# Sorted attention and a gated FFN on one core: gate weights issued one copy earlier, a narrower spreading matrix, and a new order of the last key, value and score steps of the first batch

## The chip, the core and the metric

The kernel runs on one NeuronCore of a Trainium2 chip. The core has TensorE for matmuls (weight loads are listed apart as PEld), VectorE (DVE), ScalarE (ACT), GpSimd (POOL) and SyncE (SP), and 16 DMA engines. The metric is device time in microseconds (us) of one execution. Before the change it is 244.59 us, the median of three runs (244.46 to 245.49). All times inside the text that have no other unit are us from the start of the profiled span.

## The reference

Four batches of eight heads hold 768 rows of 64 in eight blocks of 96 rows. A small 8x8 matrix per head is made doubly stochastic by five rounds of exponential, row normalisation and column normalisation. It mixes whole blocks of keys and of values, then each block of queries attends to its mixed block, and the result goes through a gated feed-forward layer of width 1536.

```
P = sort_net                                  # [4, 8, 8, 8]
for _ in range(5):
    P = exp(P - max(P)); P /= sum(P, rows); P /= sum(P, columns)
k_sorted = einsum('bhij,bhjcd->bhicd', P, k)  # the same for v
attn = softmax(q @ k_sorted.T / 8) per block of 96
x = (attn @ v_sorted) as [3072, 512]
out = (silu(x @ w_gate) * (x @ w_val)) @ w_out
```

## The kernel before, in words

All matmul operands are bf16; loads from float32 cast on their way through GpSimd's DMA queue. The work has a short opening stage and a long feed-forward stage. The feed-forward (`ffn`, with `gate`, `value` and `outp`) goes in eight steps of 384 tokens, each 12 chunks of 128 gate and value columns. While one step runs, `merge` slips the attention of a later half batch between its matmuls, at due times written into the lists. TensorE's, GpSimd's, ScalarE's and SyncE's order is the order of the program text; VectorE's is too in the opening stage, up to the first exit from the manual schedule (L583), and is chosen by the planner afterwards.

The opening stage handles the first half of batch 0. GpSimd's queue holds, in this order: the loads of batch 0's values (L131, two halves), an identity matrix, the first load of queries (L168), the two halves of the keys (L175), three copies (`copy_v`, L150) that turn values from row order into column order in `vch`, and then the weights' loads: gate and value columns 0 to 256, the second load of queries, columns 256 to 512, 512 to 1024, 1024 to 1536, and then more inputs. ScalarE copies the rest of the values between the rounds of the 8x8 normalisation (L218 to L235), whose other steps are VectorE's. The memset that puts ones into the value tile of batch pair 1 (`vt_tile(1)`) lies in the third round.

The last product of the rounds (L236) writes the matrix eight times side by side into `p_bf`. For each of eight rows two matmuls with 64 columns (L494) then spread it over 128 partitions of `w_ps`, and VectorE makes block mixing matrices `rmix` of it. Value chunks (`v_chunk`, matmuls at L300, eight or sixteen of the 64 value columns each) and key chunks (`k0_chunk`, matmuls at L284, eight or sixteen rows each) multiply by `rmix`, and a cast on VectorE ("v", L242) or ScalarE ("s", L244) moves each out of PSUM. The last two key chunks cast their first 16 blocks at once and the rest later. Then come the scores (`qk`, L332, with the exponentials at L343 or L345), the value products (`av`, L359, with a reciprocal L363 and a product L365 on VectorE), the transposes (`x_first`, L376) and the first gate and value matmuls (`early`, L559). `fill` and `wide_fill` (L477, L481) are matmuls on zeros whose results nobody reads.

PSUM has eight banks, given out under tags: "gen" is three banks in rotation, "x" one, "a" and "b" a pair of banks each. A tile under a tag waits until the last reader of the tile that held the bank is done. `k0_chunk` with 16 rows takes a pair, with eight rows one bank. `qk` under "gen" takes two single banks and makes two exponentials of 384 elements; under "a" or "b" it takes the pair and makes one of 768.

## Time and profile before

| | |
|---|---|
| median of three runs | 244.59 us (244.46, 244.59, 245.49) |
| the profiled execution | 243.93 us, span 242.2 |
| TensorE busy | 232.7 us, 96% of the span |
| VectorE busy | 155.6 us, 64% |
| ScalarE busy | 112.0 us, 46% |
| GpSimd busy | 54.9 us, 23% |
| granted TensorE clock | 1.000 |
| DMA | 24.76 MB, 102 GB/s in the mean |

The page of the profile cuts the span into 40 slices of 6.05 us and gives each engine's busy share in tenths. Its chain is the work that ended last, followed back from the end. A timeline line gives the start, the length, the engine, the line of the kernel, the operation, the output and inputs, their shape, a count where several are merged, and in brackets the idle time before it with what ended that. The list of waits gives the total, the count and the longest.

### The profile page before, as it was taken

To read this page: it belongs to the slowest core of one execution; us is meant where nothing else is said; L and a number is where in the kernel's file an instruction comes from. 1 tells how busy PE (TensorE), PEld (TensorE's weight loads), DVE (VectorE), ACT (ScalarE), POOL (GpSimd) and SP (SyncE) were. 2 spreads that over 40 slices of the span, in tenths; PEclk is the share of its full clock that TensorE was granted. 3 is DMA by queue.
4 is the path that set the end of the run, shared out by engine and by line. 5 is a ranking of instruction groups with operands and counts; after the bars stand their busy time and mean duration, and the time that the engine had idled before them with its cause. 6 is when DMAs were issued, how large, how long until landed. Compare 5 with 4: busy or idle time off the path is not lost.

```text
span 242.2 us, 5881 instructions
## 1 busy us (share of the span) xinstructions
PE 232.7 (96%) x2453; PEld 136.8 (56%) x2476; DVE 155.6 (64%) x327; ACT 112.0 (46%) x190; POOL 54.9 (23%) x66
## 2 busy tenths in 40 slices
PE   7789999999999999999999999999999999999994
PEld 3376665775556556555555565565556555555543
DVE  6796889874666585776855765484566477445700
ACT  3977652577526434455454253345325433332212
POOL 5997228970006089000000000000000000000000
PEclk9999999999999999999999999999999999999999
DMA  5989999999936999462122112012111211110122
GB/s 96 214 120 181 206 213 211 206 211 202 174 92 132 186 164 152 90 129 71 37 72 63 35 43 77 3 60 64 35 41 55 67 37 43 43 43 3 43 87 87
DMA packets 40698, 24.76 MB, mean 102 GB/s; under 512 B 29408, under 2 KB 35424, under 8 KB 40672
## 3 DMA queue, kind: packets, MB, share of 16 engines
q0 software_dynamic: 20688, 14.16, 41.2%
q1 hardware_dynamic: 19840, 10.17, 16.7%
q8 instruction: 19, 0.31, 0.5%
q10 hardware_dynamic: 144, 0.07, 0.1%
q14 instruction: 7, 0.06, 0.1%
HBM read 28.32 MB, written 7.86 MB: 149 GB/s over the span
## 4 chain that ended last, share of the span: by engine, by line
PE 85%; DMA 7%; POOL 5%; issue 1%; DVE 1%; ACT 0%; POOLq 0%
PE v_ps L428 25%; PE g_ps L410 25%; PE o_ps L445 24%; DMA wv_sb<-in_moe_w_val_dram 5%; POOL vch L150 3%; PE tkq L264 3%; PE av_ps L359 3%; PE qk L332 2%; DMA v<-in_v_dram 2%; PE tv L310 1%; PE o_ps L461 1%; POOL wg_sb L136 1%; PE tv L300 1%; POOL wv_sb L136 1%; PE x_ps L376 0%
## 5 line engine op out<-in xcount | busy, mean ns | idle before, releaser
L420 DVE SCALAR_TENSOR_TENSOR gs_sb<-th_sb,g_ps 128x384 bf16<-128x384 bf16 x96 | 52.9, 551 | 50.1 <-ACT th_sb L418 47.1
L410 PE MATMUL g_ps<-xt,wg_sb 128*128 128x384 bf16 x376 | 76.6, 325 | 0.1
L428 PE MATMUL v_ps<-xt,wv_sb 128*128 128x384 bf16 x376 | 76.5, 326 | 0.1
L418 ACT ACTIVATE th_sb<-g_ps 128x384 bf16<-128x384 f32 x96 | 47.1, 491 | 57.0 <-PE g_ps L410 54.3
L445 PE MATMUL o_ps<-wo,h 128*128 128x512 bf16 x254 | 61.4, 379 | 1.5 <-issue 0.5
L433 DVE SCALAR_TENSOR_TENSOR h<-v_ps,gs_sb 128x384 bf16<-128x384 f32 x96 | 53.4, 556 | 7.7 <-DVE gs_sb L420 0.5
L428 PEld LDWEIGHTS <-wv_sb 128*128 128x128 bf16 x376 | 35.0, 97 | 23.3 <-issue 0.2
L410 PEld LDWEIGHTS <-wg_sb 128*128 128x128 bf16 x376 | 34.9, 97 | 23.4
L445 PEld LDWEIGHTS <-h 128*128 128x128 bf16 x276 | 26.0, 98 | 28.5
L450 ACT COPY o_sb<-o_ps 128x512 f32<-128x512 f32 x23 | 13.5, 586 | 49.3 <-PE o_ps L445 49.3
L150 POOL COPY vch<-v 64x1536 bf16<-64x1536 bf16 (+2 forms) x11 | 29.4, 2712 | 9.8 <-PE g_ps L410 8.1
L345 ACT ACTIVATE e_all<-qk 96x768 bf16<-96x768 f32 x30 | 23.2, 801 | 3.8 <-PE qk L332 3.7
L365 DVE TENSOR_TENSOR st<-av_ps,r_sb 96x512 bf16<-96x512 f32 x32 | 21.8, 680 | 0.3
L359 PEld LDWEIGHTS <-e_all 96*128 96x128 bf16 x256 | 11.9, 97 | 4.6 <-ACT e_all L345 0.3
L359 PE MATMUL av_ps<-vt,e_all 96*128 96x65 bf16 x256 | 13.0, 193 | 0.2 <-ACT e_all L345 0.2
L244 ACT CAST vt<-tv 96x1024 bf16<-96x1024 f32 (+1 forms) x10 | 9.7, 965 | 4.9 <-PE tv L310 3.5
L363 DVE RECIPROCAL r_sb<-av_ps 96x8 f32<-96x8 f32 x32 | 6.4, 199 | 7.8 <-PE av_ps L359 7.8
L242 DVE CAST vt<-tv 96x1024 bf16<-96x1024 f32 (+1 forms) x8 | 8.0, 1016 | 2.1 <-PE tv L310 1.8
L481 PE MATMUL idle_ps<-wide_sb 128*128 128x512 f32 x8 | 6.4, 954 | 1.5 <-DVE wide_sb L70 1.5
L242 DVE COPY oq_v<-o_ps 128x128 f32<-128x128 f32 x1 | 0.3, 293 | 9.3 <-PE o_ps L461 9.3
L395 POOL DMA_DIRECT2D q_scr<-in_q_dram x2 | 5.6, 2813 | 0.3 <-issue 0.3
L332 PE MATMUL qk<-kqt 64*128 64x96 bf16 x128 | 4.5, 204 | 0.7 <-PE tv L300 0.4
(87 smaller groups left out, 130.8 us busy)
## 6 DMA issues: line engine op xcount, KB each, us to landing
out_dram<-o_sb SPq DMA_DIRECT2D x23, 256.0 KB, 2.0
v<-in_v_dram POOLq DMA_DIRECT2D x4, 384.0 KB, 11.7
wo<-in_moe_w_out_dram POOLq DMA_DIRECT2D x3, 512.0 KB, 16.7
kqp<-in_k_dram POOLq DMA_DIRECT2D x2, 768.0 KB, 10.3
q_scr<-in_q_dram POOLq DMA_DIRECT2D x2, 768.0 KB, 18.4
v<-in_v_dram POOLq DMA_DIRECT2D x2, 768.0 KB, 9.7
wg_sb<-in_moe_w_gate_dram POOLq DMA_DIRECT2D x2, 512.0 KB, 11.9
wv_sb<-in_moe_w_val_dram POOLq DMA_DIRECT2D x2, 512.0 KB, 14.3
```

What stands on the lines that cost most here:

```text
L150: eng.tensor_copy(dst, src.transpose([0, 2, 1]))
L244: nc.scalar.copy(dst, src)
L345: nc.scalar.activation(e_all[:, n:n + 2, 0:4 * C], wide[0:C, :, 0:4 * C], AF.Exp, scale=scale)
L359: nc.tensor.matmul(o[:, two, i4, 0:D + 1], lhsT=e[:, i4 * C:i4 * C + 128], rhs=vt[:, 2 * g + two, half * 4 + i4, 0:D + 1], start=True, sto ...
L365: nc.vector.tensor_tensor(st.rearrange("p i two d -> p two i d"), o[0:C, :, :, 0:D], r_sb.to_broadcast([C, 2, 4, D]), op=ALU.mult)
L410: nc.tensor.matmul(g_ps, lhsT=wg_sb[:, kc, ts(m, 128)], rhs=xt[:, kc, :], start=(kc == 0), stop=(kc == NKC - 1))
L418: nc.scalar.activation(th_sb, g_ps, AF.Tanh, scale=0.5)
L420: nc.vector.scalar_tensor_tensor(gs_sb, th_sb, 1.0, g_ps, op0=ALU.add, op1=ALU.mult)
L428: nc.tensor.matmul(v_ps, lhsT=wv_sb[:, kc, ts(m, 128)], rhs=xt[:, kc, :], start=(kc == 0), stop=(kc == NKC - 1))
L433: nc.vector.scalar_tensor_tensor(h_tiles[n][:, m, :], v_ps, 0.5, gs_tiles.pop(m), op0=ALU.mult, op1=ALU.mult)
L445: nc.tensor.matmul(o_ps, lhsT=h_w[:, m, ts(t3, 128)], rhs=wo_sb[part][:, m % 4, :], start=(m == 0), stop=(m == NFC - 1))
L450: nc.scalar.copy(o_sb, o_ps)
```

## The change

There are three groups of edits, all in the opening stage.

The load of gate columns 0 to 256 is issued ahead of GpSimd's third copy, and the value columns 0 to 256 stay behind that copy.

The matrix is written four times side by side for eight, and four matmuls with 32 columns do what two with 64 did. The memset of the second value tile moves from the third round to the end of the opening stage. Among the matmuls on zeros, the second group has two wide ones for one wide and three short.

The last 16 key rows go into one tile of two banks, with one cast of their first half on ScalarE and one of the rest on VectorE, where two tiles of one bank had two casts each. Value chunk 56 comes first, then 40; the first scores come next, and value chunk 48 after them. The value chunk of 16 columns is thereby cut into two of eight. One short matmul on zeros is gone, and the tags change: the first scores, the first value product and the second value product are under "b", the second and the fourth scores under "gen", the third under "a".

```diff
@@ -175,8 +175,9 @@
     copy_v(nc.gpsimd, 0, lowr, 0)
     copy_v(nc.gpsimd, 0, lowr, 3)
+    load_w(wg_sb, wg_dram, 0, 256)
     copy_v(nc.gpsimd, 0, lowr, 0, d0=40, cs=slice(46, 72))
-    load_gv(0, 256)
+    load_w(wv_sb, wv_dram, 0, 256)
     load_q0(1)
@@ -204,7 +205,7 @@
-    p_bf = const.tile([BH, NB, 8, NB], BF16)
+    p_bf = const.tile([BH, NB, 4, NB], BF16)
@@ -222,7 +223,6 @@
             copy_v(nc.scalar, 0, lowr, 0, cs=slice(24, 34))
-            vt_tile(1)
@@ -233,8 +233,8 @@
-    nc.vector.tensor_tensor(p_bf, p_ps.unsqueeze(2).to_broadcast([BH, NB, 8, NB]),
-                            colred.unsqueeze(1).to_broadcast([BH, NB, 8, NB]), op=ALU.mult)
+    nc.vector.tensor_tensor(p_bf, p_ps.unsqueeze(2).to_broadcast([BH, NB, 4, NB]),
+                            colred.unsqueeze(1).to_broadcast([BH, NB, 4, NB]), op=ALU.mult)
@@ -482,16 +482,15 @@
-    wide_fill(1)
-    fill(idle_ps, 3)
+    wide_fill(2)
...
-        for g in range(2):
-            nc.tensor.matmul(w_ps[64 * g:64 * g + 64, i].rearrange("p b h -> p (b h)"),
+        for g in range(4):
+            nc.tensor.matmul(w_ps[32 * g:32 * g + 32, i].rearrange("p b h -> p (b h)"),
@@ -524,21 +523,20 @@
-    rest = [k0_chunk(32, 8, "s", "x", 2 * NB), k0_chunk(40, 8, "v", "gen", 2 * NB)]
-    v_chunk(0, 40, 16, "v", "b")
+    drain_rest = k0_chunk(32, 16, "s", "a", 2 * NB)
     v_chunk(0, 56, 8, "s", "gen")
-    for drain_rest in rest:
-        drain_rest("v")
-    fill(pair_tile("idle_ps", "a")[:, 0:512], 1)
-    qk(0, 0, "a")
-    qk(0, 1, "b")
-    av(0, 0, "a")
-    qk(0, 2, "gen")
+    v_chunk(0, 40, 8, "v", "gen")
+    qk(0, 0, "b")
+    v_chunk(0, 48, 8, "v", "x")
+    drain_rest("v")
+    qk(0, 1, "gen")
+    av(0, 0, "b")
+    qk(0, 2, "a")
     idle_ps = bank_tile("idle_ps", "x")
     fill(idle_ps, 1)
     av(0, 1, "b")
     xts[(0, 0)] = xtp.tile([128, H2, TW], BF16, name="xt0_0", tag="xt")
-    qk(0, 3, "mixed")
+    qk(0, 3, "gen")
@@ -579,6 +577,7 @@
     q0_chunk(1, 16, 8, "v", "x")
+    vt_tile(1)
     nc.vector.tensor_copy(rmix[1][lowr, 1].rearrange("p h i -> p (h i)"), ident[lowr, lowr])
```

## The prediction

> **What bounds the kernel now.** I read the page first, for the shape of the span and the chain that ended last:

> ```profile
> PE   7789999999999999999999999999999999999994
> ...
> DMA  5989999999936999462122112012111211110122
> ...
> PE 85%; DMA 7%; POOL 5%; issue 1%; DVE 1%; ACT 0%; POOLq 0%
> ```

> TensorE is full from the fourth slice on (a slice is 6.05 us), and 85% of the chain is its own work. All that the change touches lies in the first 27 us. The chain in order of time says what releases the full stretch:

> ```profile
> 1.27 4.94 DMA v<-in_v_dram
> 6.20 0.05 issue
> 6.26 6.81 POOL vch L150 x3
> 13.07 0.71 POOL wg_sb L136
> 13.78 0.75 POOL wv_sb L136
> ...
> 17.27 12.12 DMA wv_sb<-in_moe_w_val_dram
> 29.39 0.04 issue
> 29.44 0.82 PE v_ps L428 x4
> ```

> The reader is to see GpSimd's three copies, then the weight loads issued behind them, then value weights (columns 512 to 1024) that land at 29.39, just ahead of their first matmul. But the list of waits prices that last link at little:

> ```profile
> PEld L428 <- DMA wv_sb<-in_moe_w_val_dram: 0.2, 1, 0.2
> ```

> So two paths run level: the loads, and TensorE's own work, which would have reached that matmul at 29.22. Only what shortens both moves the end. The table by stage shows where the loads lose time (columns: stretch, length, busy time of each engine, granted clock, DMA share, GB/s):

> ```profile
> 12.50:13.00 0.50, 0.50 (x22) 0.50 (x20) 0.38 (x2) 0.50 (x1) 0.50 (x2) 1.00 0.27 49
> ...
> 13.50:14.00 0.50, 0.35 (x18) 0.26 (x16) 0.50 (x1) 0.50 (x1) 0.50 (x2) 1.00 0.00 0
> 14.00:14.50 0.50, 0.50 (x43) 0.50 (x39) 0.50 (x2) 0.50 (x2) 0.50 (x1) 1.00 0.17 19
> ...
> 15.00:16.00 1.00, 1.00 (x53) 0.96 (x46) 1.00 (x3) 0.85 (x2) 1.00 (x3) 1.00 1.40 185
> ...
> 22.00:29.40 7.40, 7.38 (x109) 4.51 (x106) 5.29 (x12) 4.11 (x8) 2.30 (x4) 1.00 1.27 205
> ```

> The DMA engines stand nearly idle from 12.8 to 14.5 and are full afterwards. For TensorE's own path I took the timelines of TensorE and of VectorE, then ScalarE's:

> ```profile
> 13.84 1.93 PE L284 MATMUL tk<-rmix,qk 128*64 128x64 bf16 x96
> 15.70 0.87 PE L300 MATMUL tv<-rmix,vch 64*128 64x64 bf16 x24
> 16.95 0.35 PE L332 MATMUL qk<-kqt 64*128 64x96 bf16 x8 [0.38 <-PE tv L300]
> 17.65 0.35 PE L332 MATMUL qk<-kqt 64*128 64x96 bf16 x8 [0.35 <-DVE vt L242]
> 18.20 0.42 PE L359 MATMUL av_ps<-vt,e_all 96*128 96x65 bf16 x8 [0.20 <-ACT e_all L345]
> ```

> ```profile
> 18.65 0.20 DVE L363 RECIPROCAL r_sb<-av_ps 96x8 f32<-96x8 f32 x1 [0.39 <-PE av_ps L359]
> 18.89 0.69 DVE L365 TENSOR_TENSOR st<-av_ps,r_sb 96x512 bf16<-96x512 f32 x1
> 19.50 0.20 DVE L363 RECIPROCAL r_sb<-av_ps 96x8 f32<-96x8 f32 x1
> ```

> The gaps before 18.65 are what a new order can win. From 18.65 VectorE's normalisations follow one another (0.85 each), ScalarE's exponentials run beside them, and the first gate matmul starts at 21.05; from there TensorE has no gap worth naming up to the 29.4 wait. The line of the second key half's load sets the start of the key chunks: issued at 4.05, with the longer of

> ```profile
> DMA to landing us min/median/max: 8.3/9.0/9.6
> ```

> it lands at 13.7, and the first key matmul is at 13.84.

> **The change part by part.**

> *Gate weights ahead of the third copy.* No instruction is added. The second copy ends at 11.86, so the issue (0.79) moves from 12.99 to 11.8, the third copy (1.28) to 12.5 to 13.8, and the value weights' issue stays at 13.76, as do q0 and all that follows in GpSimd's queue. The loads take 3.8 from issue to landing with an idle queue: 16.8 becomes 15.6. The next load's packets come 1.5 after its issue (12.99 to 14.5 before), at 15.3, as the first's end; so the idle stretch shrinks by 1.1 to 1.2 and every later load, in a full queue, lands that much earlier: the 29.39 becomes about 28.25. On the path this is worth the wait and no more: 0 to 0.22, I take 0.20, since TensorE asks at 29.2. The third copy is read first by the value chunk at column 56, at 15.5 or later: 1.7 of cover; without it each us of lateness would be a us of TensorE. The second key half's last packets start before 13.0 and the moved weights' first at 13.3, behind them in the same queue: 0, bounds 0 to 0.1.

> *The four-fold matrix, the memset, the fills.* The reduction that had the ones-memset beside it took 0.356 against 0.211 elsewhere: 0.14 off the iterations, less what ScalarE's copy ending at 7.51 keeps (bounds 0.03 and 0.14). The product into p_bf has 256 elements for 512: from 0.678 (512) and 0.220 (64), 1.02 ns per element, it takes 0.42, 0.26 less. p_bf is done near 10.92 for 11.32. The spread takes 32 matmuls of 32 columns for 16 of 64. The 16 started within 0.25, two by two; the 32 take between the same (four side by side) and twice that. I take twice, so the mixing rows come 0.15 to 0.4 earlier. On TensorE it buys nothing: the key chunks still wait for the 13.7 landing. On VectorE the third value cast ends near 14.5 for 14.68, so the fourth key chunk starts at 14.60, behind its predecessor, for 14.73. The second wide fill (two records 0.43 apart) for three short ones (0.22 apart) ends near 9.5, ahead of q0's landing (9.84): 0. The memset put back behind the q0 cast at 26.8 costs VectorE 0.08 (a 0.165 copy there lets its successor start 0.08 later); the bank that it holds up is asked for later than that: 0, at most 0.1.

> *Last keys in one tile, scores between value chunks.* TensorE: fourth key chunk 14.60; the 16-row chunk (32 matmuls, 0.50) 14.85 to 15.35; with 0.13 for the change of shape, value chunk 56 at 15.48, 40 at 15.72, done at 16.12. The one short fill that goes, with its load and two shape changes, held the first scores from about 16.5 to 16.95. ScalarE takes the first halves of the 16-row tile in one 512-element cast (0.59 where a 256 took 0.37): 15.55 to 16.14. First scores 16.19 for 16.95. Their exponential: 16.56 to 17.36 (before to 18.14). VectorE has three 512-element casts (0.68 each, 0.60 apart) in a row: chunk 40 at 16.15, chunk 48 at 16.84 (its matmuls follow the first scores, done at 16.81), the second key halves 17.44 to 18.12. The first value product can start at 17.57, so its reciprocal goes at 18.05 for 18.65: 0.6 won, all of it on this step.

> Then it is given back. In the old order the first two value products lie in tags a and b; in the new both lie in b. The second must wait until VectorE has read the first: reciprocal 18.05, product to 18.97, second value product at 19.02, its reciprocal 0.45 later (18.20 to 18.65 in the rows) at 19.47, for 19.50 before. Queued behind it in TensorE's order are the fourth scores (19.36 for 19.39), whose exponentials (19.74 for 19.77) stand ahead of ScalarE's first transposed copy, which releases the first gate matmul: 21.02 for 21.05. VectorE's later pairs go 0.03 earlier too. The third scores wait for the second key halves (18.17 for 18.55), which is hidden. Bounds: 0.15 earlier (a tenth quicker in the casts) to 0.57 later (nothing won ahead of 18.65, with the serial pair kept).

> Sum: 0.03 + 0.20 = 0.23 off. The profiled execution took 243.93 (span 242.2, 1.7 around it), so 243.7; it stands 0.66 under the median of the runs shown, 244.59, from which the same sum gives 244.36, rounded to 244.3.

> **The rivals.**

> *The serial pair costs.* Break-even is a first reciprocal at 18.08, and I have it at 18.05. For: three casts in a row on VectorE, each waiting for a chunk that waits for another engine. Against: 0.6 of gaps are really there. With nothing won before 18.65 the gate matmuls start 0.57 later; with the load wait gone that is 0.35 net, 244.95.

> *A cold TensorE, on the slower side.* The first wide fills start 0.85 apart, those after 8.2 only 0.43 apart, at a granted clock that the page shows as full: the early matmuls ran at half rate. The place is 16 to 19.4: a short fill goes and the new order leaves gaps of up to 0.5, so TensorE streams some 40% of that time for nearly half before. Were the rate halved again, 3 to 5 us of dense matmuls (the cold stretch here lasted at least 5.3) would take double: 1.5 to 2.5 lost, 246.1 to 247.1, after the 0.2 won about 246.4. It decides from the point where a gap or a thin stretch is long enough; the gaps of 0.4 to 0.8 at 6.8, 10.9 and 16.6 before did not do it. [...]

> *More gain from the loads.* The runs are 0.5 to 1.6 above the profiled one; if a part of that is weights landing later than 29.39, the 1.1 that the loads gain pays for up to 0.9 more: 243.4. For: later loads are near their use as well (the last value weights land at 35.3 for 36.1). Against: nothing shows landings outside the profile.

> *The change does not do what it says.* If the moved issue's packets wait all the same, the loads land as before and the wait stays: 244.6.

> **How the numbers follow.** My forecast 0.50, the serial pair 0.22, more gain 0.12, cold TensorE 0.08, no effect 0.08. Time 244.3. The range 243.5 to 245.2 takes in the forecast with its bounds, the serial pair, no effect and most of the gain; it leaves out the cold clock and the tails. Half a per cent, 1.2 us, is about what a measurement of this kernel can tell from no change. Faster by that needs nearly all of the extra load gain: 0.07. Slower by that is the cold clock and a tail: 0.11. The rest, 0.82, is the same.

> **What would show it.** The first gate weights landing at 15.6, the value weights of 512 to 1024 near 28.3, no wait at the fifth value matmul. The p_bf product at 0.42. Key matmuls still at 13.8. First scores near 16.2, the first reciprocal near 18.05, then an idle VectorE until 19.5 with the second value product waiting for it. The first gate matmul at 21.0. I am wrong if that start moves by more than 0.3 either way, if key matmuls move, if TensorE's matmuls in the 20s take double, or if later stages show waits that were not there.

## The result and the profile after

The changed kernel takes 246.34 us, the median of 13 runs (245.56 to 249.1), against 244.59 us for the kernel before (244.05 to 245.74, 13 runs on the same chip). The ratio after to before is 1.007, with a 95% interval of 1.0044 to 1.0096: slower by 0.7%, where no measurable change was forecast. The profiled execution took 245.73 us with a span of 244.0, so the span grew by 1.8.

The page of the profile after, its slices (6.1 us each) and its chain by engine:

```profile
PE   7779999999999999999999999999999999999994
...
PEclk9997999999999999999999999999999999999999
DMA  5999999999926998644121212012111211110122
...
PE 89%; DMA 4%; DVE 3%; issue 1%; POOL 1%; ACT 0%; DVEq 0%; POOLq 0%
```

The new thing is the 7 in the fourth slice of the row of the granted clock. The clock's records in this trace say more exactly: full from the first record, at 6.20, until 19.85, half from 19.85 to 23.26 (3.41 long), full from there to the end. The profiled execution of before has no such stretch. It is no accident of one execution: the mean granted clock was 0.993 or lower in all 13 runs (3.41 at half rate in a span of 244 give 1 - 0.5 x 3.41/244 = 0.993). In five of the 13 it was 0.986 or lower, which by the same sum is two such stretches or more; these runs took 246.82 to 249.1, the other eight 245.56 to 246.56.

The chain of waits in order of time (start, length, engine, what, line) shows where the first 31 us now go:

```profile
4.04 9.65 DMA qk<-in_k_dram
...
13.83 1.58 PE tk L284 x89
15.41 0.22 issue
...
19.48 0.40 PE av_ps L359 x8
...
28.05 0.60 DVE kqt L242
28.65 0.20 issue
28.85 0.37 DVE rmix L581
29.22 0.45 DVE gs_sb L420
...
29.71 0.81 PE v_ps L428 x4
```

GpSimd's copies and the weights are gone from this chain: its first long piece is the load of the second key half, whose landing (13.69) did not move, and it runs over TensorE's opening work. At its end a value matmul waits for VectorE, through a copy and a product that stand around the moved memset. It is the fourth value chunk (some of the expectations below call it the fifth); the fifth, which had waited for weights before, follows at 31.27, long after they landed (29.50). In the list of waits this is one line:

```profile
PE v_ps L428 <- DVE gs_sb L420: 0.5, 1, 0.5
```

The table by stage (stretch, length, busy of TensorE, its weight loads, VectorE, ScalarE and GpSimd, granted clock, DMA share, GB/s) answers the one shown of before. The last row is before's for the stretch from 16.5 to 19.8:

```profile
13.50:14.00 0.50, 0.17 (x11) 0.20 (x13) 0.50 (x2) 0.50 (x1) 0.50 (x2) 1.00 0.77 79
...
15.00:16.00 1.00, 0.78 (x39) 0.66 (x33) 0.85 (x2) 0.44 (x2) 1.00 (x3) 1.00 0.70 87
16.50:19.80 3.30, 2.20 (x49) 1.63 (x49) 2.77 (x5) 2.85 (x6) 3.30 (x6) 1.00 1.21 196
19.80:23.30 3.50, 3.50 (x43) 2.67 (x41) 2.58 (x6) 2.04 (x5) 3.10 (x22) 0.51 1.32 179
```

```profile
16.50:19.80 3.30, 2.37 (x55) 1.89 (x54) 2.84 (x7) 2.96 (x6) 3.30 (x6) 1.00 1.16 175
```

Three things are to be seen. The idle DMA stretch from 13.5 on is filled (0.77 for 0.00, and 1.24 for 0.17 in the next half microsecond), but a new one stands at 15 to 16 (0.70 where before had 1.40), so most of the load's gain is given back at once. The row 16.5 to 19.8 is thin on TensorE (busy 2.20 of 3.30), but before's is nearly as thin by this measure (2.37); what tells the two apart comes further down. In the row after it the clock is 0.51 and TensorE counts as busy throughout (3.50 of 3.50): it is slow, not waiting.

TensorE's timeline over the disputed stretch, and VectorE's:

```profile
15.63 0.29 PE L284 MATMUL tk<-rmix,qk 128*64 128x64 bf16 x7 [0.22 <-issue]
16.60 0.34 PE L332 MATMUL qk<-kqt 64*128 64x96 bf16 x8
17.95 0.40 PE L359 MATMUL av_ps<-vt,e_all 96*128 96x65 bf16 x8 [0.55 <-DVE vt L242]
19.48 0.40 PE L359 MATMUL av_ps<-vt,e_all 96*128 96x65 bf16 x8 [0.26 <-DVE st L365]
21.75 0.51 PE L557 MATMUL g_ps<-xt,wg_sb 128*128 128x384 bf16 x1
```

```profile
18.41 0.19 DVE L363 RECIPROCAL r_sb<-av_ps 96x8 f32<-96x8 f32 x1
...
19.91 0.20 DVE L363 RECIPROCAL r_sb<-av_ps 96x8 f32<-96x8 f32 x1 [0.59 <-PE av_ps L359]
...
28.85 0.37 DVE L581 COPY rmix<-ident 64x64 bf16<-64x64 bf16 x1 [0.20 <-issue]
28.92 0.74 DVE L420 SCALAR_TENSOR_TENSOR gs_sb<-th_sb,g_ps 128x384 bf16<-128x384 bf16 x1
29.05 0.17 DVE L196 MEMSET vt<- 96x128 bf16 x1
```

The second value product waits for VectorE's reading of the first (19.48), so the first two reciprocals are 1.50 apart where before had 0.85. The first gate matmul starts at 21.75 (before 21.05) and, with its neighbours, takes double (0.51 for 0.32). Around the memset the cast that ends at 28.65 is followed by the end of the product only at 29.66, 1.01 later; before, the same two stood at 26.88 and 27.42, 0.54.

One sum for the span of these two executions, in starts: the first reciprocal is 0.24 earlier (18.41 for 18.65), the second 0.41 later (19.91 for 19.50), the first gate matmul 0.70 later, the second queries' matmuls 1.36 later (25.64 for 24.28), the scores behind them 1.49 later (28.71 for 27.22), the fourth value chunk 2.05 later (29.71 for 27.66), the fifth 1.83 later (31.27 for 29.44), the last instruction 1.81 later. So 0.41 is the serial pair, 0.95 comes in the steps that hold the half-rate stretch, 0.69 (of it the wait of 0.49) in the steps behind the memset, and 0.22 is won back where before had waited for weights. After 31 nothing more is lost or won.

### The profile page after: what moved, and what is told of

It is laid out like the page before. It is cut to its first block, busy times and chain, and to the rows that moved or that the text cites. A ratio compares the mean times of both kernels' runs of the same rounds, so it can differ in the third digit from the quotient of the medians.

```text
span 244.0 us, 5910 instructions
## 1 busy us (share of the span) xinstructions
PE 233.9 (96%) x2468; PEld 137.6 (56%) x2490; DVE 155.2 (64%) x326; ACT 112.4 (46%) x190; POOL 54.8 (22%) x66
## 3 DMA queue, kind: packets, MB, share of 16 engines
q1 hardware_dynamic: 19840, 10.17, 15.9%
## 4 chain that ended last, share of the span: by engine, by line
PE 89%; DMA 4%; DVE 3%; issue 1%; POOL 1%; ACT 0%; DVEq 0%; POOLq 0%
PE v_ps L428 25%; PE g_ps L410 25%; PE o_ps L445 24%; DMA qk<-in_k_dram 4%; PE av_ps L359 3%; PE tkq L264 3%; PE qk L332 3%; PE tv L310 1%; PE o_ps L461 1%; PE tv L300 1%; PE tk L284 1%; PE x_ps L376 1%; DVE h L433 1%; PE g_ps L557 1%; PE v_ps L557 1%
## 5 line engine op out<-in xcount | busy, mean ns | idle before, releaser
L420 DVE SCALAR_TENSOR_TENSOR gs_sb<-th_sb,g_ps 128x384 bf16<-128x384 bf16 x96 | 53.1, 553 | 50.4 <-ACT th_sb L418 47.3
L428 PE MATMUL v_ps<-xt,wv_sb 128*128 128x384 bf16 x376 | 76.5, 326 | 0.5 <-DVE gs_sb L420 0.5
L428 PEld LDWEIGHTS <-wv_sb 128*128 128x128 bf16 x376 | 35.1, 97 | 23.5 <-issue 0.7
L445 PEld LDWEIGHTS <-h 128*128 128x128 bf16 x276 | 26.0, 98 | 28.5
L450 ACT COPY o_sb<-o_ps 128x512 f32<-128x512 f32 x23 | 13.5, 586 | 49.3 <-PE o_ps L445 49.3
L150 POOL COPY vch<-v 64x1536 bf16<-64x1536 bf16 (+2 forms) x11 | 29.5, 2720 | 9.9 <-PE g_ps L410 8.1
L345 ACT ACTIVATE e_all<-qk 96x768 bf16<-96x768 f32 x30 | 23.3, 801 | 4.1 <-PE qk L332 4.1
L365 DVE TENSOR_TENSOR st<-av_ps,r_sb 96x512 bf16<-96x512 f32 x32 | 21.8, 681 | 0.3
L359 PEld LDWEIGHTS <-e_all 96*128 96x128 bf16 x256 | 12.4, 100 | 5.3 <-ACT e_all L345 0.6
L359 PE MATMUL av_ps<-vt,e_all 96*128 96x65 bf16 x256 | 13.5, 196 | 0.8 <-DVE vt L242 0.5
L363 DVE RECIPROCAL r_sb<-av_ps 96x8 f32<-96x8 f32 x32 | 6.4, 199 | 8.2 <-PE av_ps L359 8.2
L242 DVE CAST vt<-tv 96x512 bf16<-96x512 f32 (+1 forms) x9 | 8.1, 920 | 2.6 <-PE tv L310 1.8
L481 PE MATMUL idle_ps<-wide_sb 128*128 128x512 f32 x10 | 7.2, 866 | 1.5 <-DVE wide_sb L70 1.5
L242 DVE COPY oq_v<-o_ps 128x128 f32<-128x128 f32 x1 | 0.3, 292 | 9.3 <-PE o_ps L461 9.3
L332 PE MATMUL qk<-kqt 64*128 64x96 bf16 x128 | 4.7, 208 | 0.4 <-DVE kqt L242 0.2
## 6 DMA issues: line engine op xcount, KB each, us to landing
wg_sb<-in_moe_w_gate_dram POOLq DMA_DIRECT2D x2, 512.0 KB, 11.8
wv_sb<-in_moe_w_val_dram POOLq DMA_DIRECT2D x2, 512.0 KB, 14.5
```

Of the source, the lines that this page charges most:

```text
L150: eng.tensor_copy(dst, src.transpose([0, 2, 1]))
L332: nc.tensor.matmul(pss[two][:, i4 * C:(i4 + 1) * C], lhsT=k_sb[lo:lo + D, k_at + at:k_at + at + 128], rhs=q_sb[lo:lo + D, q_at + at:q_at + ...
L345: nc.scalar.activation(e_all[:, n:n + 2, 0:4 * C], wide[0:C, :, 0:4 * C], AF.Exp, scale=scale)
L359: nc.tensor.matmul(o[:, two, i4, 0:D + 1], lhsT=e[:, i4 * C:i4 * C + 128], rhs=vt[:, 2 * g + two, half * 4 + i4, 0:D + 1], start=True, sto ...
L365: nc.vector.tensor_tensor(st.rearrange("p i two d -> p two i d"), o[0:C, :, :, 0:D], r_sb.to_broadcast([C, 2, 4, D]), op=ALU.mult)
L420: nc.vector.scalar_tensor_tensor(gs_sb, th_sb, 1.0, g_ps, op0=ALU.add, op1=ALU.mult)
```

## The experiments

Fifteen more kernels ran. A row gives the median, the ratio to the kernel before run on the same chip with its 95% interval, in how many of its runs the mean granted clock fell to 0.994 or lower (a half-rate stretch), and from the profiled execution the first gate matmul and the landing of value weights 512 to 1024.

| run | edit | median us | ratio | half rate | gate | weights |
|---|---|---|---|---|---|---|
| after | the change | 246.34 | 1.007 (1.0044 to 1.0096) | 13 of 13 | 21.75 | 29.50 |
| e1 | after, memset back | 245.82 | 1.0041 (1.0011 to 1.0071) | 6 of 6 | 22.73 | 30.49 |
| e2 | after, four more fills | 245.82 | 1.0050 (1.0016 to 1.0084) | 2 of 6 | 24.56 | 28.72 |
| e3 | before, new order | 244.91 | 0.9992 (0.9964 to 1.0020) | 3 of 6 | 22.00 | 30.83 |
| e4 | e2 and alternating banks | 245.13 | 1.0017 (0.9986 to 1.0047) | 1 of 6 | 21.88 | 29.05 |
| e5 | before, gate weights early | 245.44 | 1.0027 (0.9999 to 1.0056) | 6 of 7 | 22.17 | 28.52 |
| e6 | before, four-fold matrix | 244.84 | 0.9993 (0.9962 to 1.0023) | 2 of 10 | 21.04 | 29.81 |
| e7 | after, eight-fold back | 247.35 | 1.0090 (1.0054 to 1.0126) | 4 of 4 | 22.07 | 29.25 |
| e8 | before, 16 tiny matmuls | 244.39 | 0.9981 (0.9961 to 1.0000) | 0 of 10 | 21.16 | 31.18 |
| e9 | e3 and two fills | 244.94 | 0.9997 (0.9979 to 1.0016) | 2 of 12 | 23.46 | 29.80 |
| e10 | e9 and alternating banks | 244.72 | 0.9992 (0.9971 to 1.0013) | 3 of 12 | 21.10 | 29.98 |
| e11 | e10 and gate weights early | 244.79 | 0.9985 (0.9966 to 1.0005) | 2 of 12 | 23.01 | 30.38 |
| e12 | before without two fills | 245.18 | 1.0011 (0.9986 to 1.0036) | 7 of 10 | 21.26 | 30.36 |
| e13 | after, three things undone | 245.31 | 1.0000 (0.9977 to 1.0024) | 2 of 12 | 21.91 | 30.68 |
| e14 | before, memset moved | 245.00 | 1.0007 (0.9983 to 1.0030) | 0 of 12 | 21.45 | 29.92 |
| e15 | before without one fill | 245.18 | 1.0008 (0.9983 to 1.0033) | 2 of 12 | 21.01 | 30.89 |

The kernel before had such a clock in 13 of the 97 runs that stood beside e1 to e15, about one in eight. Where in these runs the stretch lay is not known.

**e1: the memset back.** The first theory was that the 0.5 wait at 29.7 is the moved memset's.

```diff
         if it == 2:
             copy_v(nc.scalar, 0, lowr, 0, cs=slice(24, 34))
+            vt_tile(1)
...
-    vt_tile(1)
```

> The changed kernel with only the ones-memset put back into the third round. Theory: in its new place the memset costs VectorE 0.4 us of start-up and 0.17 of work between the query cast and the gate product, and TensorE waits 0.49 us for that product at 29.7; put back, the wait is gone and the span is about 0.5 us shorter than the changed kernel's 244.0, so 243.4 to 243.6, still slower than before because the cold stretch stays. Rival (my prediction's 0.08 for the memset): the wait stays or turns into another and the span stays within 0.15 of 244.0.

The wait of the fourth value chunk was gone, so the wait is the memset's. The ratio fell from 1.0070 to 1.0041, and the two intervals overlap; every run still had a half-rate stretch. The profiled one had two in a row (18.80 to 25.62). It also showed a wait that no theory had, in TensorE's timeline:

```profile
16.32 0.29 PE L285 MATMUL tk<-rmix,qk 128*64 128x64 bf16 x7 [1.02 <-issue]
```

**e2 and e4: fills put in, and pairs of banks in turn.** e2 adds four short matmuls on zeros to the changed kernel, between 17.2 and 19.4; e4 adds three, and lets the value products alternate between the pairs a and b.

```diff
     qk(0, 1, "gen")
+    idle_ps = bank_tile("idle_ps", "x")
+    fill(idle_ps, 2)
     av(0, 0, "b")
+    fill(idle_ps, 1)
     qk(0, 2, "a")          # e4: "gen"
-    idle_ps = bank_tile("idle_ps", "x")
-    fill(idle_ps, 1)
+    fill(idle_ps, 2)       # e4: 1
     av(0, 1, "b")          # e4: "a", then "b", "a"
```

> The changed kernel with four more short matmuls on zeros in TensorE's idle places between 17.2 and 19.4 (two before the first value product, one before the third scores, one more before the second value product). Theory: the half rate from 19.85 to 23.26 follows a thin window (42% streaming from 16.4 to 19.85); with about 65% in it the granted clock stays 1.000 and the span shrinks by 0.8 to 1.0, to 243.0 to 243.2. Rival (the half rate comes from the time or from something else than how full the window is): the clock stays at 0.993 and the span at 244.0 or more, since the fills can only delay.

> The second kernel of this call with the first four value products alternating between the two pairs of banks (b, a, b, a) as the scores allow: third scores in two single banks, fourth in one single and the x bank, the first early value matmul in b, a query chunk in a. Theory: the second value product no longer waits for the first one's normalisation, its reciprocal comes 0.85 after the first one and not 1.5, and the first gate matmul is 0.4 to 0.6 earlier than with the fills alone: span 242.5 to 242.7. Rival (the serial pair is not what is late): no earlier than with the fills alone.

Half rate fell from all runs to 2 of 6 and 1 of 6. The profiled execution of e2 is one of its two, and its half rate lay from 7.82 to 11.23, ahead of everything that the fills touch; from 11.23 on its clock was full. So with the thin stretch filled the clock stayed full in 4 of 6 and 5 of 6 runs, where the changed kernel had it in none of 13. e2 stayed 0.5% above before, e4 0.2%, which is inside its interval. The memset's wait stood in both (0.49 and 0.50). The first value product came at 18.82 in e4 for 17.95: 0.44 of that had been lost at the key tile (16.07 for 15.63), and the rest went to the fills in bank x, which had to wait for a cast themselves (0.55, ahead of the one at 18.39). And the profiled execution of e2 waited 1.73 for nothing that the profile shows, in the middle of the same 16-row key tile as e1. In e4 the first two reciprocals came to 1.06 apart, from 1.50.

**e3, e5, e6: one part of the change alone.** The new order of the last steps; the gate weights' issue ahead of the third copy; the four-fold matrix with its fills; each in the kernel before, as in the diff of the change.

> The kernel before with only the new order of the last keys, values and scores. Theory: this part alone holds the cold stretch and the serial pair: clock 0.993, first gate matmul 0.4 to 0.7 later than 21.05, nothing of the memset's 0.5; less 0.2 of the load wait that is then hidden: span 243.3 to 243.6 for 242.2. Rival (the loss is in the other two parts): span within 0.3 of 242.2 and clock 1.000.

> The kernel before with only the first gate weights' issue ahead of the third copy. My prediction: first gate weights land at 15.6, the value weights of columns 512 to 1024 near 28.3 for 29.39, span 0.2 shorter (242.0). What the changed kernel's trace suggests instead: the first gate weights land near 16.4 and the later loads within 0.2 of their old times, so the span stays within 0.15 of 242.2, clock 1.000. In both, no wait of TensorE near its 449th instruction, which it reaches at 15.9.

> The kernel before with only the four-fold matrix (16 more matmuls with their weight loads, 32 instructions more in TensorE's stream). Theory (instruction supply): in all traces so far TensorE stands still at the same place of its stream, the 449th record, until 2.5 to 3.0 us after a 16 KB instruction packet starts at 13.1 to 13.6; the 32 instructions more bring it there at 15.3 for 15.95, so a wait with no releaser of 0.2 to 1 appears there (at the fourth of the eight-row key chunks or just behind), and the first gate matmul is 0 to 0.4 later than 21.05. Rival (the wait belongs to the 16-row key tile): no such wait here.

The four-fold matrix shows no difference (0.9993), and the wait of 0.2 to 1 that e6's expectation had was 0.08. The new order alone has the half rate in 3 of 6 runs, and these show its price in one kernel: 243.99, 244.01 and 244.47 at full clock, 245.35 to 245.56 with the half-rate stretch, a difference of the medians of 1.4. The moved weights alone have it in 6 of 7 runs, where both views in the expectation had a clock of 1.000 and no wait. What is new in TensorE's timeline of e5 is a wait of 0.5 between value chunks that the kernel before does not have:

```profile
16.58 0.62 PE L301 MATMUL tv<-rmix,vch 64*128 64x64 bf16 x16 [0.50 <-issue]
```

In every trace the wait, where there is one, stands at the same place of the instruction stream: ahead of the 446th of TensorE's matmuls and weight loads (the expectations, which count other records too, call it the 449th). And in each of these traces a packet of 16 KB of the instruction queue starts 2.3 to 3.3 us ahead of the instruction that waited. In the nine traces where the gate weights are late, this packet took 0.93 to 1.08 (1.35 in e9), and TensorE was held up by 0.1 at most (by 0.45 in e14, where the packet started at 14.06 and not at 13.1 to 13.7). In the eight where they are early, their own packets run at the same time (the DMA share is 0.77 at 13.5 to 14.0 for 0.00). In six of these the packet took 1.08 to 1.93, and the delay from one start to the next was 0.4 (after), 0.5 (e7), 0.7 (e5), 1.0 (e4) and 1.2 (e1 and e13). In e2 and e11 it took 0.96 but started only at 15.8, and the delay was 1.9 and 1.4; in both a half-rate stretch lay ahead of it. In all ten traces with a delay, e14 and e6 (0.08) among them, the instruction that waited started 1.1 to 1.5 after the packet's end; in the seven without one TensorE came to the place 1.4 to 3.1 after it. That TensorE waited for the instructions in the packet is my reading of these times; no record names it, and it was not shown. What sets the start of the packet was not found.

**e7 and e8: is it the number of instructions?** The four-fold matrix adds 32 instructions ahead of the place of the wait. e7 takes them out of the changed kernel, e8 adds 16 tiny matmuls (8 columns, on zeros, with their weight loads) to the kernel before.

```diff
+    for _ in range(16):
+        nc.tensor.matmul(idle_ps[0:8, 0:8], lhsT=warm_sb[:, 0:8], rhs=warm_sb[:, 0:8], start=True, stop=True)
```

> The changed kernel with only the eight-fold matrix and its 16 matmuls put back. Theory (instruction supply): TensorE comes to the 449th record after 16.0 and the wait of 0.41 at 15.6 is gone or under 0.1, the first scores come at 16.3 for 16.60; the memset's 0.49 wait at 29.7 stays, and the clock still halves once (the order alone did it): span 243.4 to 243.8 for 244.0. Rival (the wait comes from the load order or the new tile): a wait without releaser in the key chunks stays.

> The kernel before with 16 matmuls of 8x8 on zeros put into TensorE's idle time before the first queries land (9.3 to 9.9). They cost no time there by themselves. Theory (instruction supply): they move everything behind them by 32 instructions in the stream, so TensorE reaches the 449th record near 15.4 and waits there without a releaser for 0.2 to 0.6, as in the changed kernel, though nothing else is changed; the end is 0 to 0.4 later. Rival (the wait hangs on the matrix, the tile or the loads): no wait, span within 0.1 of 242.2.

The shifted index alone does not make the wait: e7 still waited 0.49 at the place, with the packet at 1.79, and had the half rate in 4 of 4 runs; e8 did not wait and had it in none of 10. But e8 came to the place only at 15.55, 1.48 after its packet's end, so it does not show that an earlier arrival costs nothing. e5 and e7 came there at 15.9 and 15.8, as before did, so by this reading their delay is the long packet's (1.93 and 1.79), which ran beside the weights' packets. In the changed kernel the packet took only 1.08, and TensorE was there at 15.25, since the 32 added instructions stand ahead of the place: at before's 15.95, 1.8 after the packet's end, I estimate that it would have had no delay, since the traces without one came there 1.4 to 3.1 after it. There, by this estimate, the earlier arrival is the larger part.

**e9, e10, e11: the new order with its thin stretch filled.** These start from the kernel before with the new order. e9 adds two fills in a "gen" bank behind the second scores, e10 lets the value products alternate as well, e11 also issues the gate weights early.

```diff
     qk(0, 1, "gen")
+    fill(bank_tile("idle_ps"), 2)
     av(0, 0, "b")
-    qk(0, 2, "a")          # e10, e11
+    qk(0, 2, "gen")
...
-    av(0, 1, "b")
+    av(0, 1, "a")          # then "b", "a"; the third score tile "gen", the fourth "mixed"
```

> The kernel before with the new order alone (as in the order-only run), and two short matmuls on zeros behind the second scores; nothing else. Theory of the thin window: TensorE's share of the window that ends near 19.5, weighted by the rows of the array in use, rises from the .32 of the order-only run to .40 or more, so the granted clock stays at 1.000 and the gate matmuls start some 0.8 earlier than the 22.0 of the order-only run; the second value product still waits for VectorE's reading of the first (first to second reciprocal 1.5). Rival, that the new order itself (its waits) brings the half rate: a half-rate stretch of 3.4 us stays and the mean clock is 0.993.

> The run with the new order and the two short fills, and the value products in alternating pairs of banks (b, a, b, a). If the shared pair makes the 1.5 between the first two reciprocals, it falls to 0.85 here, and the gate matmuls start 0.4 to 0.6 earlier than with the shared pair, at 20.5 to 20.9. The end then depends on the loads, which land as before (29.4 or later): 0 to 0.5 below the kernel before, about 244.4. If the banks don't make it, the 1.5 and the start stay.

> The run with fills and alternating pairs, and the gate weights issued ahead of the third copy. The weights land some 0.9 earlier (value weights 512 to 1024 near 28.5). Theory that the weights' packets slow TensorE's instruction packet: the packet that starts near 13.2 takes 1.1 to 1.9 for 0.93, and TensorE waits 0.1 to 1.0 at its 449th record, near 16. Both nearly cancel: 244.0 to 244.7, and if the wait thins the window to below .38 the half rate is back in a part of the runs. Rival, that the wait comes from the longer program of the changed kernel: no such wait here, and 0.5 to 0.9 below the run without the moved weights.

With fills the new order has the half rate in 2 of 12, 3 of 12 and 2 of 12 runs, no more than the kernel before by these numbers, and the medians are those of the kernel before. The profiled execution of e9 was one of the two. Its clock fell at another place, 12.84, and stayed down for two windows, in the table by stage:

```profile
12.90:19.60 6.70, 6.70 (x173) 6.33 (x170) 4.48 (x8) 4.94 (x8) 6.70 (x11) 0.50 0.91 121
```

So the gate start of 23.46 says nothing on e9's expectation; its pair of reciprocals does: 20.39 and 21.91, still 1.52 apart. In e10 they are at 18.46 and 19.55, 1.09 apart and not the 0.85 expected. The third scores and a fill stand ahead of the second product in before too, but in e10 these scores waited 0.20 for an exponential on ScalarE (18.60). It is shown that the shared pair made most of the gap. The start of the gate matmuls, 21.10, is no earlier than before's 21.05: the 0.19 won at 18.65 is used up by the second product, so even without the shared pair the new order wins nothing there. In e11 the wait at the place was back (1.4), but not as expected: the packet was not slow (0.96), it started late (15.8), behind a half-rate stretch from 8.32 to 11.73. The loads were no earlier (30.38), and the time is the same.

**e12 and e15: the fills taken out of the kernel before.** The counter-test, with no new order, no moved load, no memset. e12 leaves out both single fills, e15 only the one that the change dropped.

```diff
-    fill(pair_tile("idle_ps", "a")[:, 0:512], 1)     # e12 and e15
...
-    idle_ps = bank_tile("idle_ps", "x")              # e12
-    fill(idle_ps, 1)
```

> The kernel before without its two single short matmuls on zeros (near 16.5 and 18.8); nothing that the output needs is left out. Theory of the thin window: the weighted share of the window falls from .43 to about .31, the clock halves for 3.4 us in most runs, mean clock 0.993, and the time is 1 us or more longer. [...]

> The kernel before without the one short fill near 16.5, which the change dropped too; the other stays. If the window's share alone decides, it falls from .43 to about .38, between the shares that halved the clock (.34 and less) and those that kept it (.39 and more): half rate in a third to two thirds of the runs, fewer than the 7 in 10 without both fills, 0 to 0.5 above the kernel before. If the change's half rate in all runs came of the dropped fill alone, it is here in all runs, and 1 above.

e12 is the plainest result of the study. Two matmuls whose results nobody reads are gone, and 7 of 10 runs have a half-rate stretch, where the kernel before, run beside it, had one in 4 of 35: median 245.22 with it, 244.36 without (three runs), 0.9 apart. The longest idle time of TensorE in the 3.41 ahead of it is under one microsecond:

```profile
17.86 0.35 PE L332 MATMUL qk<-kqt 64*128 64x96 bf16 x8 [0.91 <-DVE vt L242]
```

Taken over all runs, the median is only 0.1% above before, inside its interval, and not the 1 or more that was expected. The first scores start 0.35 earlier (16.60 for 16.95), which may make up for a part; that was not separated. e15 had the half rate in 2 of 12 runs, like the kernel before, fewer than expected. The dropped fill alone is not the cause; in the change the serial pair and the wait at the key tile come on top of it, and e3 and e5 fit that.

**e13 and e14: is that all?** e13 is the changed kernel with three things undone: two fills behind the second scores, alternating pairs, the memset back (the edits of e1 and e10 together). Early gate weights, four-fold matrix and new order stay. e14 is the kernel before with the memset alone moved.

> The changed kernel with three things undone: the memset back in the third round, two short matmuls on zeros behind the second scores, the value products in alternating pairs of banks. The moved gate weights, the four-fold matrix and the new order stay. Theory that thin window, memset and shared pair make the whole loss: clock 1.000 in most runs, first to second reciprocal 0.85, no wait at the fifth value matmul for the cast behind the memset, 244.4 to 245.0, like the kernel before. Rival, that the longer program or the moved weights cost TensorE by themselves: 0.5 to 1 above the kernel before.

> The kernel before with the memset alone moved to the end of the opening stage. If it costs 0.5 of VectorE's time there (0.4 before it starts and 0.17), the cast at L420 ends near 28.2 for 27.4, still ahead of the weights' landing at 29.4: 0 to 0.3 above the kernel before, and the third round is 0.4 to 0.6 shorter. Rival, that the memset is worth its whole 0.5 by itself: 0.5 above.

e13 has a ratio of 1.0000 (0.9977 to 1.0024), 10 of 12 runs at full clock, and no wait for VectorE at the fourth value chunk: the three things together are the loss, within the 0.25% of the interval. Its first reciprocals were 1.08 apart, not 0.85. It still had the wait at the key tile, at 16.48 for 1.03, as e1 had. In this execution that did not set the end, since at 30.7 TensorE waited 0.49 for weights. That this wait matters through the clock, because it thins the stretch, is what e5 suggests; it was not tried alone. Mended like this, the change wins nothing. e14 is no slower than before: the product behind the memset takes as long as in the changed kernel (0.75), and TensorE waits 0.22 for it at 28.4, but the fifth chunk's weights (29.92) come later than that anyway. The third round won less than expected: from the first reciprocal of the rounds to the product into `p_bf` e14 took 7.65 for 7.80, so 0.15 and not 0.4 to 0.6. The 0.5 is a cost only where TensorE's path sets the end.

**What separates the windows.** All half-rate stretches in these traces ahead of the last microseconds are 3.41 or 6.83 long, they begin a whole number of 3.41 after the first record of the clock (four in the changed kernel, from 6.20 to 19.85), and their phase against the program differs from run to run (the first record is at 6.46 in before). That the clock goes by windows of 3.41 that run free of the program is my reading of this; no record shows how it is set. For each window of the 17 traces that began at full clock before 21.5 I summed the streaming time of TensorE's matmuls (columns times 0.42 ns, from gate matmuls of 384 columns that start 0.16 apart), weighted by the rows of the array that are in use, side-by-side matmuls on the same rows counted once, as a share of the window. The wide fills are not bf16 but float32, and start 0.43 apart at full clock; with that for each of them the first windows of before and of the changed kernel come to 0.44 and 0.54, and both were followed by full clock. Of 9 windows with a share of 0.34 or less, 8 were followed by half rate (0.25 in e1, 0.31 in e2 and e7, 0.32 in e3 and e5, 0.33 in e11 and e12, 0.34 in the changed kernel). Of 67 with more, one was (0.38 in e9). The windows of e2 and e11 are early ones, which end near 8 and hold an idle time of 1.9; the others end between 18.8 and 20.6. The kernel before has 0.43 there, e15 and e14 0.35 and 0.36. It is a reading made after the fact, with one exception on each side, and the line is not sharp: when each matmul that starts in a window counts whole, the windows of e6 and e8 that end near 18.7 come to 0.34 too, and both kept the clock, while the two early ones come to 0.38. That rows count was not tested by itself. The longest idle time alone does not separate them: a window of e2 (14.65 to 18.06) held one of 1.48 and kept the clock, and in e5 the longest was 0.5.

## Why the prediction was wrong, point by point

It said 244.3 and the same with a chance of 0.82; the result, 246.34 and slower, lies outside the range of 243.5 to 245.2, in the rival that had a chance of 0.08. (The sum gave 244.36, which rounds to 244.4.)

**The step that failed: the rival "A cold TensorE", set at 0.08.** The forecast put nothing into its sum for it. The runs showed a half rate from 19.85 to 23.26 in the profiled execution, at least one such stretch in all 13 runs, and 0.95 of the 1.8 lost in the steps that hold it. The place (16 to 19.4) and the mechanism (a stretch thinned by the dropped fill and by gaps of up to 0.5) came out as that rival had them, as far as a share of 0.34 for before's 0.43 shows it, though the dropped fill alone is not enough (e15: 2 of 12 runs). That its time of about 246.4 agrees with 246.34 is luck: it priced the clock alone, and the serial pair and the memset make up the rest. What failed is the reason given for discounting it, that the gaps of 0.4 to 0.8 before "did not do it". In the changed kernel no idle time longer than 0.55 lay in the 3.41 before the rate fell, in e12 none longer than 0.91, and before kept the full clock through an idle time of 0.78 (ahead of 7.56): the longest gap alone did not decide, and the 7 of 10 runs of e12 speak for the thin stretch. The prediction had computed that TensorE streams "some 40% of that time for nearly half before" and had no row for what share is enough, so its 0.08 was the author's estimate. The price, "1.5 to 2.5 lost", was too high: 1.4 in e3, 0.9 in e12, 0.95 in the changed kernel's trace, where the stretch lasts one window of 3.41 and holds waits as well.

**The serial pair** was worked out right in its mechanism, and as a rival it came true: reciprocals at 18.41 and 19.91 for the 18.05 and 19.47 of the forecast, past the break-even of 18.08. The sum's 0.6 won ahead of the first reciprocal was 0.24. It lost about 0.4 at the key tile, which went on at 15.63, 0.41 after the matmul before, where 0.03 is usual; no step had this. First scores came at 16.60 for 16.19, the first value product at 17.95 for 17.57.

**Gate weights ahead of the third copy.** The issue moved to 11.87 (forecast 11.8) and the copy to 12.65 to 13.92, as said. The load took 4.5 from issue to landing, not the 3.8 that the forecast took from before (12.99 to 16.8): 16.37 for 15.6. The step "the idle stretch shrinks by 1.1 to 1.2" failed, since the second load's packets, still issued at 13.84, left a new thin stretch at 15 to 16. The DMA share from 13 to 17 adds to 3.73 where before has 3.26, and before's two full us from 15 to 17 have 1.40 each: 0.3 us of work gained. The value weights landed at 29.50, not 28.25. Over all profiled executions they landed at a median of 29.4 with the weights early (eight, 28.5 to 30.7) and 30.0 without (nine, 29.4 to 31.2). That scatter of 2 us between executions is the substance of the rival "More gain from the loads": kernels at full clock range over 2 us too (e14: 243.88 to 246.06, clock 0.997 or more in all 12 runs). The bound of "0 to 0.1" for the moved packets' harm was put on the key load, which indeed did not move (13.69). The instruction packet, a user of the DMA engines that the prediction had not counted, though the profile's page lists its queues, took up to 1.93 in the kernels with early weights; in the changed kernel's own trace it took 1.08 for 0.93.

**The memset.** The term of 0.08, hidden, was mis-sized: the stretch from the cast to the end of the product grew by 0.47, and in the changed kernel TensorE's fourth value chunk waited 0.49 for it. VectorE's timeline of before had a row for it: the like memset of the first value tile, at 2.47, stands with an idle time of 0.40 ahead of its 0.17, ended by nothing that the profile shows. The prediction took 0.08, from a copy. The price depends on the place: in the third round the same memset had no idle time ahead of it and cost 0.15.

**The four-fold matrix** was right in its sizes: the reduction at 0.21, the product into `p_bf` at 0.41 (0.42). `p_bf` was ready 0.29 earlier and not 0.40, since the rounds began 0.14 later in this execution (first reciprocal 2.98 for 2.84). The 32 narrow matmuls took 0.37 for the 0.42 of the 16, a little under the lower bound, so the mixing rows came 0.28 earlier, and the fourth key chunk's cast and all behind it gained nothing, as said (the key chunks wait for the 13.69 landing). In e6 the first gate matmul starts at 21.04 for 21.05, and its time is that of before within the 0.4% of its interval. The sum's 0.20 for the load wait came out for another reason than the one given: the fifth value chunk no longer waited for weights because TensorE came to it 1.83 later; the weights themselves landed 0.11 later.

## What to carry to other kernels

A matmul on zeros in a thin stretch was not waste to be cleaned away here (without two of them 7 of 10 runs of e12 had a half-rate stretch, for 4 of 35 of the kernel before): before dropping one, or before lengthening a stretch of small matmuls on part of the array, add up how much TensorE streams in a stretch of 3.41 us, the length of the half-rate stretches here, and compare with stretches that kept and lost the full clock, in several traces if there are any. When a load is moved earlier, count every queue that then shares the DMA engines with it, the instruction queue too (its packet took up to 1.93 here for before's 0.93), and look at what TensorE does after that packet's start (here the delayed instruction came 2.3 to 3.3 later). When an instruction is moved, price it at its new place, with the idle time that such a row had elsewhere (0.40 ahead of before's memset at 2.47), and not with its duration alone (0.17).
